# Clustered attention and two MLPs on one core: the first head pair in an older form, two low halves given to VectorE, and new order tables

## Chip, core and metric

The kernel runs on one core of a Trainium2 chip. The metric is the device time of one execution in microseconds (us), the median of three runs. Before the change it is 789.33 us.

## What is computed

```python
q_n, k_n, c_n = q / (|q| + 1e-6), k / (|k| + 1e-6), centroids / (|centroids| + 1e-6)
q_assign = argmax(einsum('bhsd,hcd->bhsc', q_n, c_n), -1)     # k_assign alike; 16 clusters
mask     = q_assign[:, :, :, None] == k_assign[:, :, None, :]
scores   = where(mask, q @ k.T / sqrt(D), -1e9)               # B, H, S, D = 2, 8, 768, 64
attn     = softmax(scores) @ v                                # written as x: 1536 tokens x 512
h = x @ w_in;  g = h * cos(h);                            x   = g @ w_out     # MLP1, 512-2048-512
h = x @ w_in2; g = where(h > 0, h, exp(min(h, 0)) - 1);   out = g @ w_out2    # MLP2
```

All of it is float32. TensorE multiplies fp32r values, so nearly every operand is split into a high half (a rounded copy) and a low half (operand minus high half), and three products stand for one: high by high, high by low, low by high.

## The kernel before

**Attention** goes by head pairs, two heads at a time, eight pairs in all. For a pair, the k and q rows are loaded, squared and summed, and their inverse norms come from three Newton steps on small tiles. TensorE transposes k and q, multiplies them with the normalised centroids (L874), and the argmax over 16 clusters is a chain of small VectorE and GpSimd operations on the tile `sm`: scale by the norm (L894), maximum (L902), compare (L909), keep the first (L918), a maximum again, and the one-hot tile `M` (L940). `M` is transposed and put beside k and q, so that the mask comes out of the score product itself (L1039, L1042). Each 128 queries are one step: scores, row maximum (L1047), exponential `P` (L1053), turn (L1062), halves `PH` and `PL` (L1076, L1082), times `V` (L1093). While a pair's six steps run, the next pair is prepared.

**The first pair** has no earlier pair to hide behind and has its own functions. `first_pe`, `first_hi`, `first_low` and `first_stack` make the stacked operands X0k, X0q (first head) and X1k, X1q (second head) from one transposed k or q. The centroids are normalised by `cen_sq`, fourteen small GpSimd operations (`cen_step`) and `cen_scale`. For the second pair, GpSimd and VectorE make the low halves `lo` (L742, L744), and SyncE copies the halves into X0k and X1k by DMA (L755 to L760).

**The MLPs.** The 1536 tokens are three token tiles of 512, t = 0, 1, 2. The hidden width is 16 slices f of 128. Token tile 0 goes slice by slice: `g1` (L221) is twelve matmuls giving h, `act` makes the activation and its halves GH and GL, `g2` (L280) is twelve matmuls into four accumulators. Token tiles 1 and 2 go by pairs p of slices (f = 2p and 2p+1) with seven half-size products (`prod`, L480) in place of eight, after which `post` combines them, and `act2` makes the activation and its halves. In MLP1 the activation is six operations on ScalarE and VectorE, then GH by ScalarE (L93) and GL by GpSimd (L544):

```python
        elif i == (5 if m == 0 else 3):
            copy_on(G2_ON[m][e][0], GH, A)
        else:
            eng = nc.vector if G2_ON[m][e][1] == "dve" else nc.gpsimd
            eng.tensor_tensor(out=GL, in0=A, in1=f32(GH), op=ALU.subtract)
```

Weights come from memory as 64-bit numbers. For each f, `load_w` (L144, L146) loads a raw tile through SyncE and `w_part` turns it into halves: ScalarE (L163), VectorE twice (L165, L167), then the high half (L93, L95 or L97, by engine) and the low half (L175) of a `slot`. The slot of a slice is used by all three token tiles of its MLP and then taken for the raw weights of the next. At the **boundary between the MLPs**, TensorE does the last `g2` slices of MLP1 (t = 2, f = 12 to 15) and the first `g1` slices of MLP2 in a written order. x is 512 wide, so four pieces of it are split too, XH (GpSimd, L97) and XL (VectorE, L202). The first two slots of MLP2 are made ahead in a guest place and only their halves remain.

**The order.** Every engine runs its instructions in order. Which stands where is not found by a scheduler: tables of numbers give each part a time, all parts are sorted by it, and written out in that order. FIRST holds the first pair, PAIR each later one, STEP, HALF and UNIT the attention steps, LAST the passage into MLP1, MLP and WINO the two forms of MLP tiles, WB the weight sums of the second form. OWN and the short tables ending in `_ON` name the engine of a part (MLP1's token tile 0 and the x halves above all).

## Time and profile before

| | |
|---|---|
| median of three runs | 789.33 us (786.51 to 790.74) |
| the profiled execution | 789.13 us, of which the span is 787.3 us; 1.83 us lie outside |
| TensorE matmuls (PE) | 766.7 us busy, 97% of the span |
| TensorE weight loads (PEld) | 686.5 us, beside the matmuls |
| VectorE (DVE) | 612.9 us, 78% |
| ScalarE (ACT) | 553.8 us, 70% |
| GpSimd (POOL) | 402.3 us, 51% |

The span is what the trace covers, from the first instruction to the last. Rows of the timeline give an instruction's start, its duration, its engine and line, what it writes and reads, and in brackets how long the engine had stood idle before it and who ended the idle time. Matmuls overlap, so those of 0.39 us start every 0.23 us. PEclk is the granted clock of TensorE as a share of 2.4 GHz.

The stages by time: to about 20 us the first pair is prepared, to 240 us attention runs, at 240 to 265 us attention passes into MLP1. MLP1's token tile 0 follows until about 350 us, and its tiles 1 and 2 until 521 us. The boundary between the MLPs is at 517 to 530 us, and MLP2 fills the rest.

### The profile page before, as it was taken

How to read it: one execution, taken by the hardware profiler on the slowest of the kernel's cores; microseconds unless marked ns; L12 is line 12 of the kernel's file. 1: busy time of each engine (PE TensorE's matmuls, PEld its weight loads, DVE VectorE, ACT ScalarE, POOL GpSimd, SP SyncE). 2: the span in 40 equal slices, each digit the busy share in tenths (PEclk: the TensorE clock that was granted, in tenths of full speed). 3: DMA queues.
4: the chain of work that ended last, by engine and by line, in shares of the span. 5: the costliest groups of instructions: out<-in, count | busy, mean ns of one | idle time of the engine just before them, and what ended most of it. 6: DMA issues, size and time to landing. Idle time of an engine off the chain costs nothing.

```text
span 787.3 us, 13051 instructions
## 1 busy us (share of the span) xinstructions
PE 766.7 (97%) x4579; PEld 686.5 (87%) x4579; DVE 612.9 (78%) x1008; ACT 553.8 (70%) x1035; POOL 402.3 (51%) x472
## 2 busy tenths in 40 slices
PE   6899999999999999999999999989999999999998
PEld 5789999999998878889999899968888999999996
DVE  6789899898899989989998844688978577663442
ACT  5788988989989988867666755766755554654343
POOL 7755866866865732444655422251228666532221
PEclk9899999999999999999999999999999999999999
DMA  5546657647437395011123238882000222223221
GB/s 122 121 98 154 147 117 161 138 104 182 101 87 267 39 374 210 1 40 61 62 81 121 71 113 285 292 275 102 0 1 25 110 81 82 81 95 120 81 80 54
DMA packets 72145, 93.27 MB, mean 118 GB/s; under 512 B 31440, under 2 KB 52432, under 8 KB 72080
## 3 DMA queue, kind: packets, MB, share of 16 engines
q1 hardware_dynamic: 71936, 92.41, 39.4%
q8 instruction: 36, 0.59, 0.3%
q14 instruction: 29, 0.24, 0.1%
q10 hardware_dynamic: 144, 0.03, 0.0%
HBM read 58.75 MB, written 15.78 MB: 95 GB/s over the span
## 4 chain that ended last, share of the span: by engine, by line
PE 91%; ACT 3%; POOL 2%; DVE 1%; DMA 1%; issue 1%; SPq 1%; ACTq 0%; POOLq 0%
PE a L280 32%; PE h L480 20%; PE h L221 11%; PE px L1093 8%; PE pt L1062 8%; PE s L1039 4%; PE s L1042 4%; PE pt_sim L874 2%; PE pt_raw L718 1%; ACT P L1053 1%; POOL GL L544 1%; ACT PH L1076 1%; DMA nat_q<-in_q_dram 1%; DMA X1k<-lo 1%; SPq L607 0%
## 5 line engine op out<-in xcount | busy, mean ns | idle before, releaser
L544 POOL TENSOR_TENSOR GL<-A,GH 128x512 fp32r<-128x512 f32 x64 | 93.3, 1463 | 155.2 <-ACT GH L93 118.4
L280 PE MATMUL a<-GH,slot 128*128 128x512 f32 x384 | 124.7, 393 | 0.0
L280 PE MATMUL a<-slot,GH 128*128 128x512 f32 x384 | 118.4, 389 | 0.0
L1082 DVE TENSOR_TENSOR PL<-pt,PH 128x384 fp32r<-128x384 f32 x192 | 99.0, 547 | 16.5 <-ACT PH L1076 16.5
L1076 ACT ACTIVATE PH<-pt 128x384 fp32r<-128x384 f32 x192 | 85.0, 496 | 18.5 <-PE pt L1062 18.3
L1047 DVE TENSOR_REDUCE m<-s 128x1 f32<-128x768 f32 x96 | 91.0, 948 | 4.2 <-PE s L1042 3.5
L1053 ACT ACTIVATE P<-s,m 128x768 f32<-128x768 f32 x96 | 87.3, 910 | 0.9 <-DVE m L1047 0.6
L280 PEld LDWEIGHTS a<-GH,slot 128*128 128x128 f32 x384 | 72.7, 189 | 14.8
L1062 PE MATMUL pt<-ident,P 128*128 128x128 f32 x576 | 84.2, 280 | 0.0
L221 PE MATMUL h<-XH,slot 128*128 128x512 f32 x256 | 83.7, 391 | 0.0
L280 PEld LDWEIGHTS a<-slot,GH 128*128 128x128 f32 x384 | 71.0, 188 | 14.0
L480 PE MATMUL h<-XH,slot 128*128 128x256 f32 x384 | 81.8, 282 | 0.0
L280 PE MATMUL a<-GL,slot 128*128 128x512 f32 x192 | 75.6, 394 | 3.7 <-POOL GL L544 3.7
L280 PE MATMUL a<-slot,GL 128*128 128x512 f32 x192 | 74.8, 389 | 0.0
L1062 PEld LDWEIGHTS pt<-ident,P 128*128 128x128 f32 x576 | 67.3, 142 | 6.3 <-DVE PL L1082 1.2
L93 ACT ACTIVATE GH<-A 128x512 fp32r<-128x512 f32 x86 | 53.9, 627 | 21.2 <-DVE A L539 9.3
L391 POOL TENSOR_TENSOR X<-slot 128x512 f32<-128x512 f32 x32 | 49.0, 1543 | 37.0 <-DVE sums L434 23.5
L480 PEld LDWEIGHTS h<-XH,slot 128*128 128x128 f32 x384 | 65.0, 190 | 0.7
L502 DVE TENSOR_TENSOR X<-X 128x256 f32<-128x256 f32 x32 | 23.4, 733 | 49.1 <-ACT X L500 48.9
L1093 PE MATMUL px<-PL,V 128*128 128x384 f32 x192 | 57.9, 356 | 0.7
L1093 PE MATMUL px<-PH,V 128*128 128x384 f32 x192 | 58.2, 357 | 0.0
L221 PEld LDWEIGHTS h<-XH,slot 128*128 128x128 f32 x256 | 48.2, 189 | 10.3 <-DVE slot L175 0.3
(197 smaller groups left out, 1958.6 us busy)
## 6 DMA issues: line engine op xcount, KB each, us to landing
raw<-in_moe_w_in_dram SPq DMA_DIRECT2D x32, 512.0 KB, 7.9
raw<-in_moe_w_out_dram SPq DMA_DIRECT2D x32, 512.0 KB, 8.8
sd<-sums SPq DMA_DIRECT2D x32, 384.0 KB, 2.3
sums<-sd SPq DMA_DIRECT2D x32, 384.0 KB, 3.5
nat_k<-in_k_dram SPq DMA_DIRECT2D x16, 192.0 KB, 3.3
nat_q<-in_q_dram SPq DMA_DIRECT2D x16, 192.0 KB, 3.8
nat_v<-in_v_dram SPq DMA_DIRECT2D x8, 384.0 KB, 4.4
xr<-row SPq DMA_DIRECT2D x32, 96.0 KB, 3.5
```

Of the source, the lines that this page charges most:

```text
L93: nc.scalar.activation(out=out, in_=in_, func=AF.Copy)
L221: nc.tensor.matmul(h, lhsT=a[:, kd, :], rhs=b, start=(kd == 0 and i == 0), stop=(kd == NKD - 1 and i == 2))
L280: nc.tensor.matmul(accs[m, t][e], lhsT=a, rhs=b, start=(f == 0 and i == 0), stop=(f == NF - 1 and i == 2))
L391: eng.tensor_tensor(out=u[:, i].rearrange("p e n -> p (e n)").rearrange("p (k f) -> p k f", k=NKD), in0=f32(ih), in1=f32(il), op=ALU.add)
L480: nc.tensor.matmul(o, lhsT=x[:, k], rhs=piece(y, k), start=(k == 0 and n == 0), stop=(k == 1 and n == 2))
L544: eng.tensor_tensor(out=GL, in0=A, in1=f32(GH), op=ALU.subtract)
L1047: nc.vector.tensor_reduce(out=m, in_=st[n]["s"][:, :, 0:HW], axis=AX.XY, op=ALU.max, negate=True)
L1053: nc.scalar.activation(out=P, in_=st[n]["s"][:, :, 0:HW], func=AF.Exp, bias=st[n]["m"], accum_out=den_all[:, u % NDEN, j, r, 0:1])
L1062: nc.tensor.transpose(pt[:, c * 128:(c + 1) * 128], st[n]["P"][:, e, c * 128:(c + 1) * 128], ident)
L1076: nc.scalar.activation(out=ph, in_=pt, func=AF.Copy)
L1082: nc.vector.tensor_tensor(out=pl, in0=pt, in1=f32(ph), op=ALU.subtract)
L1093: nc.tensor.matmul(tx[g][:, 0:HW], lhsT=V2s[pp][:, j, c, :], rhs=halves[g][a][:, c, :], start=(n == 0), stop=(n == 2 * C - 1))
```

## The change

Three things. **One:** the low halves GL of the last two pairs of MLP1 at t = 2 (f = 12 to 15, four instructions) are made by VectorE.

```diff
+G2_LATE = ((0,2,6), (0,2,7))
...
-            eng = nc.vector if G2_ON[m][e][1] == "dve" else nc.gpsimd
+            eng = nc.vector if G2_ON[m][e][1] == "dve" or (m, t, p) in G2_LATE else nc.gpsimd
```

**Two:** the first head pair. The centroid load goes on SyncE's queue ahead of k (it was on ScalarE's). The first pair's v is loaded ahead of the second head's k and q. The centroid's Newton steps are eleven VectorE operations (`norm_steps`) in place of GpSimd's. The low half X1q is VectorE's (it was GpSimd's, from a copy `fraw` by ScalarE), and T1k is ScalarE's (was VectorE's) and the copy X1k GpSimd's (was ScalarE's). GpSimd no longer halves the squares of the second head. VectorE does the second head's scale and keep-the-first (were GpSimd's).

```diff
-        nc.scalar.dma_start(out=cen[:, 0, :], in_=centroids.rearrange("h c d -> (h c) d"))
+        nc.sync.dma_start(out=cen[:, 0, :], in_=centroids.rearrange("h c d -> (h c) d"))
         for j in range(2):
             load_nat(0, "k", (j,))
             load_nat(0, "q", (j,))
-        load_nat(0, "v")
+            if j == 0:
+                load_nat(0, "v")
...
+        def norm_steps(key):
+            need(("seed", key))
+            ss, x, y, a = nt[key]
+            for _ in range(3):
+                nc.vector.tensor_tensor(out=a, in0=y, in1=y, op=ALU.mult)
+                nc.vector.scalar_tensor_tensor(out=a, in0=a, scalar=-0.5, in1=x, op0=ALU.mult, op1=ALU.mult)
+                nc.vector.scalar_tensor_tensor(out=y, in0=a, scalar=1.5, in1=y, op0=ALU.add, op1=ALU.mult)
+            nc.vector.tensor_tensor(out=y, in0=y, in1=ss, op=ALU.mult)
+            nc.vector.tensor_scalar_add(y, y, 1e-6)
...
-            if (w, j) == ("q", 1):
-                need(("fraw", w, j))
-                nc.gpsimd.tensor_tensor(out=xl, in0=raws_sb[0, w, j], in1=f32(th), op=ALU.subtract)
...
-            if js == (1,):
-                nc.gpsimd.tensor_tensor(out=sq[:, 1, :, 0:D // 2], in0=sq[:, 1, :, 0:D // 2], in1=sq[:, 1, :, D // 2:D],
-                                        op=ALU.add)
...
-            eng = nc.vector if js == (0,) else nc.gpsimd
+            eng = nc.vector if pp == 0 else nc.gpsimd
```

**Three:** all order tables have new numbers, and OWN new engines. In MLP1's token tile 0, the high halves of the weight slices 3, 7, 10 and 14 and the low half of slice 9 go to GpSimd, and so do GH of slices 9 and 15 and one XH; GpSimd gives up the high half of slice 8, GH of 5 and 10 and GL of 15. VectorE has three operations fewer there.

```diff
-STEP = {'qk': -0.7084, 'rowmax': -0.484, 'expo': 0.6444, 'turn:0': 1.5027, 'p_hi:0': 1.7761, 'p_lo:0': 2.025, 'turn:1': 1.6032, 'p_hi:1': 2.0128, 'p_lo:1': 2.2586}
+STEP = {'qk': -0.8439, 'rowmax': -0.5989, 'expo': 0.4499, 'turn:0': 1.4222, 'p_hi:0': 1.9292, 'p_lo:0': 2.1434, 'turn:1': 1.4486, 'p_hi:1': 1.9304, 'p_lo:1': 2.2468}
...
```

**VectorE at the boundary of the MLPs.** Before, from a middle row of the activation of f = 15 (tiles R_6693 and A_6644; those of f = 14 are R_6685 and A_6643) to the low half of MLP2's slot 2 (u is a weight on its way into a slot):

```order
L523 SCALAR_TENSOR_TENSOR R_6693<-R_6693,A_6644 128x512
L202 TENSOR_TENSOR XL_6664<-X_67,XH_6663 128x512
L533 TENSOR_TENSOR A_6643<-A_6643,R_6685 128x512
L202 TENSOR_TENSOR XL_6700<-X_67,XH_6699 128x512
L202 TENSOR_TENSOR XL_6691<-X_67,XH_6690 128x512
L165 TENSOR_SCALAR u_6717<-u_6717 128x1024
L533 TENSOR_TENSOR A_6644<-A_6644,R_6693 128x512
L175 TENSOR_TENSOR slot1_6728<-guest1_6633,slot1_6728 128x1024
L167 SCALAR_TENSOR_TENSOR u_6717<-raw2_6341,u_6717 128x1024
L165 TENSOR_SCALAR u_6749<-u_6749 128x1024
L175 TENSOR_TENSOR slot2_6751<-u_6717,slot2_6751 128x1024
```

In the change, from the same row (f = 14 is A_6642, f = 15 is A_6643):

```order
L524 SCALAR_TENSOR_TENSOR R_6690<-R_6690,A_6643 128x512
L176 TENSOR_TENSOR slot0_6668<-guest0_6518,slot0_6668 128x1024
L534 TENSOR_TENSOR A_6642<-A_6642,R_6686 128x512
L203 TENSOR_TENSOR XL_6658<-X_67,XH_6657 128x512
L203 TENSOR_TENSOR XL_6672<-X_67,XH_6671 128x512
L534 TENSOR_TENSOR A_6643<-A_6643,R_6690 128x512
L545 TENSOR_TENSOR GL_6688<-A_6642,GH_6687 128x512
L166 TENSOR_SCALAR u_6719<-u_6719 128x1024
L168 SCALAR_TENSOR_TENSOR u_6719<-raw2_6225,u_6719 128x1024
L545 TENSOR_TENSOR GL_6692<-A_6643,GH_6691 128x512
L176 TENSOR_TENSOR slot1_6723<-guest1_6600,slot1_6723 128x1024
```

GL_6688 and GL_6692 stand in VectorE's queue behind the last A and ahead of the low half of slot 1, with two rows of slice 2 between them. Behind these rows VectorE also makes the high halves of slots 2 and 3, which it did not before.

**GpSimd at the boundary.** Before, from the GL of f = 12 on:

```order
L544 TENSOR_TENSOR GL_6575<-A_6530,GH_6574 128x512
L544 TENSOR_TENSOR GL_6581<-A_6531,GH_6580 128x512
L97 TENSOR_SCALAR XH_6663<-X_67 128x512
L97 TENSOR_SCALAR XH_6690<-X_67 128x512
L97 TENSOR_SCALAR XH_6699<-X_67 128x512
L544 TENSOR_TENSOR GL_6687<-A_6643,GH_6686 128x512
L544 TENSOR_TENSOR GL_6695<-A_6644,GH_6694 128x512
L97 TENSOR_SCALAR slot2_6751<-u_6717 128x1024
L263 TENSOR_TENSOR GL_6768<-A_6765,GH_6767 128x512
```

In the change:

```order
L545 TENSOR_TENSOR GL_6466<-A_6425,GH_6465 128x512
L545 TENSOR_TENSOR GL_6470<-A_6426,GH_6469 128x512
L98 TENSOR_SCALAR XH_6653<-X_67 128x512
L98 TENSOR_SCALAR XH_6657<-X_67 128x512
L98 TENSOR_SCALAR XH_6664<-X_67 128x512
L98 TENSOR_SCALAR XH_6671<-X_67 128x512
L264 TENSOR_TENSOR GL_6758<-A_6755,GH_6757 128x512
```

The four GL after GL_6470 and slot 2's high half are gone from here, and one XH more stands in their place; the next row is a GL of MLP2.

**TensorE and GpSimd in the first pair.** TensorE before, from the scores of the fourth step (`s`) to those of the fifth; X0k and X1k here are the second pair's, whose low halves arrive by DMA:

```order
L1039 MATMUL s_454<-X0k_177,X0q_202 128x384 x2
L1042 MATMUL s_454<-T0k_179,T0q_204 128x384 x2
L874 MATMUL pt_sim_460<-CC_152,X0k_359 128x32 x4
L1062 MATMUL pt_465<-ident_121,P_436 128x128 x3
L1062 MATMUL pt_471<-ident_121,P_436 128x128 x3
L874 MATMUL pt_sim_460<-CC_152,X0k_359 128x32 x2
L874 MATMUL pt_sim_460<-CC_152,X1k_360 128x32
L1039 MATMUL s_493<-X0k_177,X0q_202 128x384 x2
L1042 MATMUL s_493<-T0k_179,T0q_204 128x384 x2
```

In the change:

```order
L1034 MATMUL s_446<-X0k_167,X0q_196 128x384 x2
L1037 MATMUL s_446<-T0k_169,T0q_198 128x384 x2
L869 MATMUL pt_sim_452<-CC_152,X0k_345 128x32 x2
L869 MATMUL pt_sim_452<-CC_152,X1k_346 128x32 x2
L1057 MATMUL pt_461<-ident_121,P_430 128x128 x3
L1057 MATMUL pt_465<-ident_121,P_430 128x128 x3
L869 MATMUL pt_sim_452<-CC_152,X0k_345 128x32
L869 MATMUL pt_sim_452<-CC_152,X1k_346 128x32 x2
L869 MATMUL pt_sim_452<-CC_152,X0k_345 128x32
L1034 MATMUL s_485<-X0k_167,X0q_196 128x384 x2
L1037 MATMUL s_485<-T0k_169,T0q_198 128x384 x2
```

A product with X1k now stands right behind the first with X0k, ahead of the turn (`pt`). GpSimd, before, ahead of the second pair's first `lo`:

```order
L996 TENSOR_SCALAR V2_332<-nat_v_113 128x6x64
L894 TENSOR_TENSOR sm_266<-sm_266,nrm_189 128x2x96
L830 TENSOR_TENSOR sq_350<-nat_k_115 128x768
L835 TENSOR_TENSOR sq_350<-sq_350 128x12x32
L838 TENSOR_TENSOR sq_350<-sq_350 128x12x16
L918 TENSOR_TENSOR sm_266<-sm_266,desc_128 128x2x96
L742 TENSOR_TENSOR lo_364<-raw_371,hi_363 128x384
```

In the change:

```order
L675 TENSOR_SCALAR ny_264<-ny_264 128x12
L828 TENSOR_TENSOR sq_358<-nat_k_115 128x768
L830 TENSOR_TENSOR sq_358<-sq_358 128x12x32
L833 TENSOR_TENSOR sq_358<-sq_358 128x12x16
L752 TENSOR_TENSOR lo_350<-raw_362,hi_349 128x384
L828 TENSOR_TENSOR sq_406<-nat_q_118 128x768
```

The V copy, the scale and the keep-the-first (the two rows on `sm`) no longer stand ahead of `lo`.

## Rows read from the trace of the kernel before

**Rows 1.** The page, busy time of TensorE: busy us, share of the span, instructions

```profile
PE 766.7 (97%) x4579; PEld 686.5 (87%) x4579; DVE 612.9 (78%) x1008; ACT 553.8 (70%) x1035; POOL 402.3 (51%) x472
```

**Rows 2.** The page, the chain that ended last, shares of the span by engine

```profile
PE 91%; ACT 3%; POOL 2%; DVE 1%; DMA 1%; issue 1%; SPq 1%; ACTq 0%; POOLq 0%
```

**Rows 3.** Windows: stretch, its us, each engine's busy us, PEclk, DMA share, GB/s

```profile
60.00:240.00 180.00, 179.43 (x1252) 169.33 (x1251) 162.34 (x319) 165.10 (x381) 122.56 (x194) 1.00 0.59 137
265.00:425.00 160.00, 160.00 (x858) 138.44 (x857) 149.56 (x216) 118.72 (x190) 72.98 (x49) 1.00 0.32 111
530.00:784.00 254.00, 253.53 (x1439) 223.14 (x1437) 163.12 (x239) 137.14 (x227) 104.23 (x72) 1.00 0.19 69
526.00:530.00 4.00, 4.00 (x12) 3.15 (x11) 2.42 (x3) 1.15 (x2) 1.55 (x2) 0.57 0.98 351
31.00:39.00 8.00, 7.80 (x35) 7.51 (x36) 5.16 (x9) 4.21 (x10) 4.59 (x16) 0.57 0.68 146
285.00:325.00 40.00, 40.00 (x178) 32.89 (x177) 39.93 (x51) 32.31 (x45) 8.23 (x6) 1.00 0.56 200
```

**Rows 4.** Waits of TensorE: total us, times, longest us

```profile
PE a L280 <- POOL GL L544: 3.7, 1, 3.7
...
PE pt_c L693 <- DVE cen L687: 1.6, 1, 1.6
```

**Rows 5.** Timeline of TensorE at the boundary of the MLPs

```profile
525.34 0.50 PE L280 MATMUL a<-GL,slot 128*128 128x512 f32 x1 [3.66 <-POOL GL L544]
```

**Rows 6.** Timeline of GpSimd: the GL of f = 14 and 15

```profile
519.71 6.83 POOL L544 TENSOR_TENSOR GL<-A,GH 128x512 fp32r<-128x512 f32 x2 [4.30 <-ACT GH L93]
```

**Rows 7.** Tile GL, 495 to 530 us: ns min/median/max, first and last start

```profile
L544 POOL TENSOR_TENSOR GL<-A,GH x6: 1283/1297/5581, 497.6 to 525.3; 128x512 fp32r<-128x512 f32 x6
```

**Rows 8.** Timeline of VectorE at the boundary

```profile
517.61 0.68 DVE L202 TENSOR_TENSOR XL<-X,XH 128x512 fp32r<-128x512 f32 x1
...
520.62 0.68 DVE L533 TENSOR_TENSOR A<-A,R 128x512 f32<-128x512 f32 x1
521.22 1.21 DVE L175 TENSOR_TENSOR slot<-guest,slot 128x1024 fp32r<-128x1024 f32 x1
```

**Rows 9.** Timeline of TensorE in the first pair

```profile
28.55 0.59 PE L874 MATMUL pt_sim<-CC,X0k 128*128 128x32 f32 x4 [1.31 <-DMA X0k<-lo]
...
31.20 0.25 PE L874 MATMUL pt_sim<-CC,X1k 128*128 128x32 f32 x1 [1.21 <-DMA X1k<-lo]
```

**Rows 10.** Timeline of GpSimd in the first pair

```profile
14.70 1.81 POOL L801 TENSOR_TENSOR X1q<-fraw,T1q 64x768 fp32r<-64x768 f32 x1
...
19.98 0.51 POOL L996 TENSOR_SCALAR V<-nat_v 128x384 fp32r<-128x384 f32 x1
20.45 0.52 POOL L894 TENSOR_TENSOR sm<-sm,nrm 128x192 f32<-128x192 f32 x1
...
24.11 0.58 POOL L918 TENSOR_TENSOR sm<-sm,desc 128x192 f32<-128x192 f32 x1
24.65 1.00 POOL L742 TENSOR_TENSOR lo<-raw,hi 128x384 fp32r<-128x384 f32 x1
```

**Rows 11.** SyncE's queue: first load, and the copy that X1k waits for

```profile
0.73 0.39 SPq L607 DMA_DIRECT2D nat_k<-in_k_dram  x1
...
26.88 0.59 SPq L758 DMA_DIRECT2D X1k<-lo  x1
```

**Rows 12.** Timeline of VectorE in the first pair

```profile
13.70 0.95 DVE L804 SCALAR_TENSOR_TENSOR X1k<-s_raw,T1k 64x768 fp32r<-64x768 f32 x1
...
17.15 0.36 DVE L909 TENSOR_TENSOR sm<-sm,mx 128x192 f32<-128x192 f32 x1
...
21.39 1.22 DVE L909 TENSOR_TENSOR sm<-sm,mx 128x192 f32<-128x192 f32 x1
```

**Rows 13.** Timeline of TensorE: g1 of two slices of MLP1 that follow each other

```profile
296.21 0.39 PE L221 MATMUL h<-XH,slot 128*128 128x512 f32 x1
...
301.65 0.39 PE L221 MATMUL h<-XH,slot 128*128 128x512 f32 x1
```

More of the change, by code (lines that the diff above doesn't have):

```diff
@@ L28 @@
-STEP = {'qk': -0.7084, 'rowmax': -0.484, 'expo': 0.6444, 'turn:0': 1.5027, 'p_hi:0': 1.7761, 'p_lo:0': 2.025, 'turn:1': 1.6032, 'p_hi:1': 2.0128, 'p_lo:1': 2.2586}
-HALF = {'av:0:0': 6.7513, 'av:0:1': 6.3384, 'av:1:0': 6.9826, 'av:1:1': 4.8875, 'av:2:0': 5.1627, 'av:2:1': 6.3004, 'av:3:0': 4.7675, 'av:3:1': 4.6933, 'av:4:0': 4.8112, 'av:4:1': 4.6976, 'av:5:0': 4.8024, 'av:5:1': 6.8253, 'x_main': 7.2376, 'x_low': 7.0237}
-UNIT = {'den_eps': 2.8361, 'recip': 3.7535, 'recip_rows': 6.6707, 'recip_out': 8.4112, 'x_add': 9.2483, 'x_mul': 17.2906}
@@ new lines @@
+STEP = {'qk': -0.8439, 'rowmax': -0.5989, 'expo': 0.4499, 'turn:0': 1.4222, 'p_hi:0': 1.9292, 'p_lo:0': 2.1434, 'turn:1': 1.4486, 'p_hi:1': 1.9304, 'p_lo:1': 2.2468}
+HALF = {'av:0:0': 6.2719, 'av:0:1': 4.8074, 'av:1:0': 4.7218, 'av:1:1': 4.4542, 'av:2:0': 6.276, 'av:2:1': 4.9696, 'av:3:0': 4.6165, 'av:3:1': 6.4759, 'av:4:0': 4.979, 'av:4:1': 6.5822, 'av:5:0': 5.1983, 'av:5:1': 6.4762, 'x_main': 7.0575, 'x_low': 6.9662}
+UNIT = {'den_eps': 2.7037, 'recip': 3.2698, 'recip_rows': 5.4033, 'recip_out': 8.9866, 'x_add': 8.4622, 'x_mul': 16.7153}
@@ L43 @@
 ABS2_ON = ("act", "act")
+G2_LATE = ((0, 2, 6), (0, 2, 7))
 GUEST = {(1, 0): 9, (1, 1): 10}
@@ L49 @@
 RAW_ON = {('k', 0): 'act', ('k', 1): 'dve', ('q', 0): 'act', ('q', 1): 'act'}
-HI2_ON = {('k', 0): 'act', ('k', 1): 'act', ('q', 0): 'act', ('q', 1): 'act'}
+HI2_ON = {('k', 0): 'act', ('k', 1): 'pool', ('q', 0): 'act', ('q', 1): 'act'}
 ZON = {'z': 'act', **{(w, h, j): 'dve' if (w, h) == ('k', 1) else 'act' for w in 'kq' for h in range(2) for j in range(2)}}
@@ L54 @@
 SQ0_ON = {('k', 0): 'act', ('k', 1): 'act', ('q', 0): 'act', ('q', 1): 'act'}
-TH_ON = {('k', 0): 'act', ('k', 1): 'dve', ('q', 0): 'act', ('q', 1): 'act'}
+TH_ON = {('k', 0): 'act', ('k', 1): 'act', ('q', 0): 'act', ('q', 1): 'act'}
 WHI_ON = {0: 'act', 1: 'act'}
@@ L649, in norm_seed @@
             made("seed", key)
+        def norm_steps(key):
[7 more added lines that the diff above has]
+            nc.vector.tensor_scalar_add(y, y, 1e-6)
+            made("steps", key)
         def norm_step(key, i):
@@ L679, in cen_sq @@
             norm_seed("c", css, "c")
-        def cen_step(i):
-            norm_step("c", i)
         def cen_scale():
@@ L787, in first_hi @@
             made("th", w, j)
-        def first_raw(w, j):
-            raw = raws_sb[0, w, j] = pre.tile([64, 2, HW], F32, tag="fraw", bufs=1, name="fraw")
-            src, sc, *_ = first_parts(w, j)
-            nc.scalar.activation(out=raw, in_=src, func=AF.Copy, scale=sc)
-            made("fraw", w, j)
         def first_low(w, j):
@@ L798, in first_low @@
             src, sc, th, xh, xl = first_parts(w, j)
-            if (w, j) == ("q", 1):
-                need(("fraw", w, j))
-                nc.gpsimd.tensor_tensor(out=xl, in0=raws_sb[0, w, j], in1=f32(th), op=ALU.subtract)
-                made("low", w, j)
-                return
             nc.vector.scalar_tensor_tensor(out=xl, in0=src, scalar=sc, in1=f32(th), op0=ALU.mult, op1=ALU.subtract)
@@ L846, in sum_sq @@
             nc.vector.tensor_reduce(out=sss[pp][:, "kq".index(w), cols(js)],
-                                    in_=sqs[pp, w, js][:, cols(js), :, 0:(D // 2 if js == (1,) else D if pp == 0 or SS_ON[w] == "dve" else D // 4 if SSQ == "quarter" else D // 2)],
+                                    in_=sqs[pp, w, js][:, cols(js), :, 0:(D if pp == 0 or SS_ON[w] == "dve" else D // 4 if SSQ == "quarter" else D // 2)],
                                     axis=AX.X, op=ALU.add)
@@ L916, in sims_first @@
             sm = sims_of(pp, js)
-            eng = nc.vector if js == (0,) else nc.gpsimd
+            eng = nc.vector if pp == 0 else nc.gpsimd
             eng.tensor_tensor(out=sm, in0=sm, in1=desc.unsqueeze(1).unsqueeze(1).to_broadcast(list(sm.shape)),
@@ L1199 @@
                 fn, own = named(name)
-                if fn in (first_pe, first_hi, first_raw, first_low, first_hi2, first_stack):
+                if fn in (first_pe, first_hi, first_low, first_hi2, first_stack):
                     at(time, fn, *own, j)
@@ L1203 @@
                     at(time, fn)
-                elif fn is cen_step:
+                elif fn is norm_steps:
                     at(time, fn, *own)
```

14 lines of the change are left out of this document (7 added, 7 removed).

## The prediction

> **What bounds the kernel now.** I read the page first. TensorE computes in 766.7 us of a span of 787.3 us [rows 1], so 20.6 us of idle time is all that an order can win, apart from time at a lower clock. The chain that ended last is TensorE for 91% [rows 2]. A change that moves work among the other engines pays only where TensorE waits for that work, and costs only where it makes TensorE wait. So I looked by stage for idle time. Steady attention leaves 0.57 us in 180, the MLP1 stretch none in 160, MLP2 0.47 us in 254 [rows 3]. What is left lies at the two ends of the order: the first pair, and the boundary of the MLPs.
>
> At the boundary there is one wait of 3.66 us for a low half GL by GpSimd [rows 4, 5]. The reader should see why it is long. GL has a median of 1.30 us, and the one that TensorE waits for took 5.58 [rows 7]; it begins at 519.71 [rows 6], with VectorE's operations back to back beside it [rows 8]. The second of the two rows grouped there took only about 1.25 us. After the wait TensorE works at a granted clock of 0.57 for 4 us [rows 3], between the levels 2.4 and 1.2 GHz, having been idle just before. That costs 4 x (1 - 0.57) = 1.7 us more. In the first pair the second pair's keys come late by DMA, with waits of 1.31 and 1.21 us [rows 9], and behind them 8 us pass at 0.57 [rows 3], or 8 x 0.43 = 3.4 us lost.
>
> **The change part by part.** The sum starts from the profiled execution, 789.13 us, of which 1.83 lie outside the span.
>
> *The two late GL.* They leave GpSimd for VectorE. For one on VectorE the nearest row is a subtraction of the same shape and kinds, 0.68 us, of which a run of them starts every 0.6 [rows 8]. Where they stand decides. Before, A of f = 15 starts at 520.62 [rows 8]; one weight row of 0.6 that stood ahead of it is behind it now, and slot 0's low half has only changed places within the run. So A ends at about 520.7 and the GL of f = 14 at about 521.4. TensorE wants it 3.66 us ahead of 525.34, at 521.68 [rows 5]. Allowing for the wait on GH, the remaining stall is 0 to 0.4; I take 0.3. Two rows of slice 2 follow (together about 1.8), then the GL of f = 15, done at 523.9 to 524.3. TensorE comes to it one g2 later. A slice's g1 and g2 together take 301.65 - 296.21 = 5.44 us [rows 13], so g2 half of that, and the need is at 521.68 + 2.7 = 524.4. Slot 1's low half takes 1.21 [rows 8] and ends by 525.5. Its need, after both g2, is about 521.5 + 5.4 = 526.9. All hold, the tightest by 0.1 us. The gain is 3.66 - 0.3 = 3.4, the bounds 0 and 3.66. With no idle time of that size ahead of it, I expect no fall of the clock: 1.7 more, the bounds 0 and 1.7.
>
> *What GpSimd no longer does there* covers nothing else: it stands idle 4.30 us ahead of these GL [rows 6]. The extra XH fits in that.
>
> *The second pair's keys.* GpSimd's `lo` starts at 24.65. The V copy, 0.51, the scale, 0.52, and the keep-the-first, 0.58, leave its queue, 1.6 us in all, and X1q, 1.81, makes place for a plain copy [rows 10]. I take 2.0, since behind that `lo` waits for ScalarE's halves. The DMA copy X1k, issued at 26.88 [rows 11], should follow and land at about 29.2, not 31.2 [rows 9]. But TensorE now asks for X1k right behind X0k, before the turn, and not behind it. It came to X0k at 28.55 - 1.31 = 27.24 [rows 9], so one idle stretch of 29.2 - 27.24 = 2.0 us takes the place of 1.31 + 1.21 = 2.5: a gain of 0.5. Bounds: a loss of 1.4, if X1k lands no earlier (31.20 - 27.24 = 4.0 in place of 2.5, with the turn behind it), and a gain of 2.5. The clock loss of 3.4 may go with it or stay; since an idle stretch remains, I leave it in the sum.
>
> *The head up to the first scores.* The centroid load ahead of k on SyncE's queue puts k about 0.39 later [rows 11]. Against it, the centroid's Newton steps leave GpSimd for VectorE, and VectorE's X1q is a row of 0.95 [rows 12] in place of GpSimd's 1.81 [rows 10]; VectorE gives up T1k, whose row is of the same size. The wait for the centroid is 1.6 [rows 4]. I take 0. The best is half the centroid's wait, a gain of 0.8; the worst is k's delay and a second delay of the same order from v ahead of the second head, a loss of 1.0.
>
> *The second head's small operations on VectorE.* The compare L909 took 0.36 us at 17.15 and 1.22 at 21.39 [rows 12], the second time beside GpSimd's work on squares. Two more such operations now stand in VectorE's queue beside the squares, ahead of the first row maximum. I take 0, since the squares can also begin later or earlier; the bound is 0.9, one such difference. The Trainium skill's page "SBUF — State Buffer", section "SBUF: two separate sides", says that a VectorE operation with two SBUF inputs and a GpSimd one exclude each other for a whole instruction. By that rule the second head would lose those 0.9 us for certain, and the sum would be 784.4 in place of 783.5; the two prices of L909 agree with the rule, as does the GL of 5.58 us.
>
> *All other tables.* Steady attention, MLP1 and MLP2 have 0.57, 0 and 0.47 us to win [rows 3]. I take 0, with a gain of 1.0 and a loss of 3 as bounds, the loss being one new wait of the size of the boundary's without its clock.
>
> The sum: 789.13 - 3.4 - 1.7 - 0.5 = 783.5 us. The profiled execution is 0.2 below the median of the runs, so for the median I say **783.7 us**. About 0.5%, 3.9 us, is what a measurement of this kernel can tell from no change, so faster means under 785.4 and slower over 793.3.
>
> **The rivals.**
>
> *A: the clock holds in the first pair too.* If the granted clock stays at 1.00 behind the one stretch of idle time, the 3.4 come on top: 783.7 - 3.4 = 780.3. For it: one stretch in place of two. Against it: about 2.0 us of idle time remain, near the 2.5 behind which the clock fell.
>
> *B: the stall moves into VectorE's queue.* GL now waits behind A, XL and slot rows. If A is 1.5 to 2.5 us later than walked, since the sine is later on ScalarE, TensorE waits about 2.0 in place of 0.3, the clock falls as before and the 1.7 stay: 783.7 + 2.0 - 0.3 + 1.7 = 787.1, with a spread of 786 to 788.5, which is no change. For it: margins of 0.1 us; behind the GL on VectorE stand the low halves of slots 1 to 3, for which the first g1 of MLP2 wait. Against it: the times of the walk are VectorE's own of before [rows 8], and only 0.68 us for each GL is new in its queue.
>
> *C: slower, by GpSimd starved in MLP1's token tile 0.* From 285 to 325 us VectorE is busy in 39.93 of 40 us and GpSimd in 8.23 [rows 3]. The change gives GpSimd seven more pieces in that tile, and if they stand beside VectorE as the GL at the boundary did, each takes up to 5.58 - 1.30 = 4.3 us more. A slice has 5.44 us. Where GpSimd's end comes after TensorE's need, a wait like the boundary's follows, 3.66 + 1.7 = 5.4 us; two such waits give 783.7 + 10.7 = 794.4. It decides from the second late piece on. For it: the saturated VectorE. The exclusion that the Trainium skill's page "SBUF — State Buffer" states would bear on this too, wherever both read two operands at once. Against it: 31 us of GpSimd's idle time in these 40, and VectorE has three operations fewer there.
>
> **How the numbers follow.** The forecast has 0.50: its own range, with the head and the tables at part of their bounds, is 781.5 to 785.4. A has 0.15, B 0.25, C 0.10. Faster is the forecast and A, 0.65; within 0.5% is B, 0.25; slower is C, 0.10. The range holds the forecast, A and B: 780.0 to 788.5. It leaves out C and the ends of A and B.
>
> **What would show it.** At the boundary the wait of TensorE for GL should be gone or under 0.5 us, with VectorE as its releaser, and the granted clock 1.00 where it was 0.57. In the first pair, one wait for X1k, none for X0k behind the turn, and `lo` near 23 us. In the windows of attention and of both MLPs, TensorE's idle time should not grow by over a microsecond. The forecast is wrong if TensorE waits for a slot or for GL on VectorE (B), if there are waits in MLP1's first token tile for GpSimd's slot or GH (C), or if the first scores come over 1 us later.

## The result, and the profile after

| | before | changed |
|---|---|---|
| median | 789.34 us (786.51 to 790.74, 4 runs) | **778.12 us** (777.81 to 778.32, 4 runs) |
| ratio | | 0.9862, 95% interval 0.9835 to 0.9889 |
| profiled execution, span | 789.13, 787.3 us | 778.07, 776.3 us |

The change is faster by 11.2 us, twice the 5.6 that were forecast, and 1.9 us below the range. This is a difference of medians. Beside the experiments below, the kernel before ran 71 times more, from 780.8 to 791.5 us; seven of these, 780.8 to 781.8 us, have a mean granted clock of 1.000, about 3 us above the changed kernel at such a clock (777.8 to 778.3 us at 0.999 to 1.000). So most of the gain seems to lie in waits and stretches of lower clock that the kernel before has in most of its executions, but not in all. None of the seven was profiled; the rows of before come from an execution that has them. The page of the changed kernel, busy time and then the chain by engine:

```profile
PE 761.6 (98%) x4579; PEld 682.2 (88%) x4579; DVE 631.8 (81%) x1026; ACT 548.0 (71%) x1030; POOL 387.0 (50%) x453
...
PE 86%; DVE 6%; ACT 4%; DMA 2%; issue 1%; SPq 0%; POOL 0%; ACTq 0%; DVEq 0%
```

The same matmuls take 5.1 us less than in [rows 1], as much as the two stretches of lower clock cost before (1.7 + 3.4). The rest of the 11 us of span is idle time. The waits of TensorE, total us, times, longest:

```profile
PE pt_sim L869 <- DMA X1k<-lo: 1.1, 2, 0.5
...
PE pt_c L703 <- DVE cen L697: 0.7, 1, 0.7
...
PE pt_sim L869 <- ACT hi L737: 0.6, 1, 0.6
...
PE pt_sim L869 <- DMA X1q<-lo: 0.4, 1, 0.4
```

GL is not among them, and the centroid has 0.7 us in place of 1.6 [rows 4]. Windows of the changed kernel (stretch, its us, busy us of PE, PEld, DVE, ACT and POOL, PEclk, DMA share, GB/s): attention, MLP1, MLP2, and the 8 us in the first pair where the clock had been low:

```profile
60.00:240.00 180.00, 178.30 (x1237) 167.07 (x1235) 163.09 (x314) 164.52 (x375) 124.63 (x195) 1.00 0.60 144
265.00:425.00 160.00, 160.00 (x872) 139.41 (x871) 148.38 (x210) 116.45 (x184) 75.89 (x53) 1.00 0.33 116
525.00:773.00 248.00, 247.50 (x1413) 218.12 (x1411) 175.34 (x239) 131.72 (x222) 104.78 (x72) 1.00 0.20 72
28.00:32.00 4.00, 3.47 (x30) 3.38 (x28) 3.48 (x8) 3.78 (x9) 3.05 (x11) 1.00 1.05 216
32.00:36.00 4.00, 4.00 (x33) 3.75 (x30) 3.41 (x6) 3.83 (x8) 1.04 (x5) 1.00 1.00 167
```

Against [rows 3], attention has 1.1 us more idle time (two new waits for DMA copies, 0.43 and 0.51 us, are in it), the MLPs none, and the granted clock is 1.00 where it was 0.57. TensorE in the first pair, first scores and products of the second pair's keys, and then its first low half on GpSimd and the DMA copy of X1k on SyncE's queue:

```profile
18.61 0.99 PE L1034 MATMUL s<-X0k,X0q 128*128 128x384 f32 x2
...
26.41 0.40 PE L869 MATMUL pt_sim<-CC,X0k 128*128 128x32 f32 x2 [0.55 <-ACT hi L737]
27.35 0.36 PE L869 MATMUL pt_sim<-CC,X1k 128*128 128x32 f32 x2 [0.54 <-DMA X1k<-lo]
```

```profile
21.23 1.00 POOL L752 TENSOR_TENSOR lo<-raw,hi 128x384 fp32r<-128x384 f32 x1
```

```profile
23.56 0.59 SPq L768 DMA_DIRECT2D X1k<-lo  x1
```

The first scores stood at 19.85 us before. `lo` is 3.4 us earlier than in [rows 10] and X1k's copy 3.3 earlier than in [rows 11], and the two waits ahead of the products are 1.1 us where they were 2.5 [rows 9]. Only the second of them is still for a key's DMA copy; the first ends with a copy by ScalarE (`hi`). The scores of the fifth step start at 28.64, 2.66 us earlier than before, and the second pair's first scores at 48.98, where before they stood at 55.26. So the sum of the profiled executions is: 1.24 us to the first scores, 1.42 more to the fifth step and 3.62 more behind it, where the clock had been low, 6.3 in all; 3.66 + 1.7 at the boundary of the MLPs; 0.36 for a wait for XL in MLP1 that is gone; less 0.94 for the two new waits in attention. That makes 11.1, and 789.13 - 778.07 is 11.1.

VectorE at the boundary, changed kernel:

```profile
514.73 0.69 DVE L545 TENSOR_TENSOR GL<-A,GH 128x512 fp32r<-128x512 f32 x1
...
516.06 1.23 DVE L168 SCALAR_TENSOR_TENSOR u<-raw,u 128x1024 uint32<-128x1024 uint32 x1
517.20 0.69 DVE L545 TENSOR_TENSOR GL<-A,GH 128x512 fp32r<-128x512 f32 x1
517.80 1.22 DVE L176 TENSOR_TENSOR slot<-guest,slot 128x1024 fp32r<-128x1024 f32 x1
```

A GL takes 0.69 us here, and TensorE's first product with the GL of f = 14 starts at 516.05 without a wait: 0.6 us of slack, where the forecast had a wait of 0.3.

### The profile page after: what moved, and what is told of

Read it like the earlier page. It is cut to its first block, busy times and chain, and to the rows that moved or that the text cites. A ratio compares the mean times of both kernels' runs of the same rounds, so it can differ in the third digit from the quotient of the medians.

```text
span 776.3 us, 13062 instructions
## 1 busy us (share of the span) xinstructions
PE 761.6 (98%) x4579; PEld 682.2 (88%) x4579; DVE 631.8 (81%) x1026; ACT 548.0 (71%) x1030; POOL 387.0 (50%) x453
## 4 chain that ended last, share of the span: by engine, by line
PE 86%; DVE 6%; ACT 4%; DMA 2%; issue 1%; SPq 0%; POOL 0%; ACTq 0%; DVEq 0%
PE a L281 32%; PE h L481 20%; PE h L222 11%; PE pt L1057 6%; PE px L1088 6%; PE s L1034 3%; PE s L1037 3%; PE pt_sim L869 2%; DVE m L1042 2%; DVE PL L1077 1%; DMA X1k<-lo 1%; PE pt_raw L728 1%; ACT PH L1071 1%; DMA X1q<-lo 1%; ACT P L1048 1%
## 5 line engine op out<-in xcount | busy, mean ns | idle before, releaser
L545 POOL TENSOR_TENSOR GL<-A,GH 128x512 fp32r<-128x512 f32 x60 | 81.1, 1357 | 150.5 <-ACT GH L94 118.6
L281 PE MATMUL a<-GH,slot 128*128 128x512 f32 x384 | 122.9, 390 | 0.0
L481 PE MATMUL h<-XH,slot 128*128 128x256 f32 x384 | 79.2, 281 | 0.0
L501 ACT ACTIVATE X<-h 128x512 f32<-128x512 f32 x32 | 19.1, 597 | 54.2 <-PE h L481 54.0
L1088 PE MATMUL px<-PL,V 128*128 128x384 f32 x192 | 56.2, 368 | 0.0
```

The costliest lines, as they stand in the source:

```text
L281: nc.tensor.matmul(accs[m, t][e], lhsT=a, rhs=b, start=(f == 0 and i == 0), stop=(f == NF - 1 and i == 2))
L481: nc.tensor.matmul(o, lhsT=x[:, k], rhs=piece(y, k), start=(k == 0 and n == 0), stop=(k == 1 and n == 2))
L1088: nc.tensor.matmul(tx[g][:, 0:HW], lhsT=V2s[pp][:, j, c, :], rhs=halves[g][a][:, c, :], start=(n == 0), stop=(n == 2 * C - 1))
```

## Experiments

The kernel before ran beside each. Its own executions spread from 780.8 to 791.5 us, with mean granted clocks of 0.980 to 1.000 over the run, so each ratio below has an interval of about 0.3 to 0.6% either way.

### The boundary of the MLPs: GL alone, GL undone, GL seven times

**GL on VectorE alone.** The kernel before with

```diff
+G2_LATE = ((0,2,6), (0,2,7))
-            eng = nc.vector if G2_ON[m][e][1] == "dve" else nc.gpsimd
+            eng = nc.vector if G2_ON[m][e][1] == "dve" or (m, t, p) in G2_LATE else nc.gpsimd
```

> The kernel before with the four GL of f = 12 to 15 on VectorE alone; they stand where the old tables put them, behind the last A and ahead of slot 1's low half. Theory (the wait of 3.7 us was GpSimd's GL running beside VectorE): that wait gone or under 0.5 us, granted clock 1.00 behind it: 789.3 - 5 = 784.3 us. Rival (the wait moves to the slots, whose low halves now stand behind two more operations on VectorE, so that only the new tables make it pay): a wait of 1.5 to 3 us for a slot and the lower clock: 787 to 789 us.

784.95 us, ratio 0.9965 (0.9934 to 0.9996). TensorE at the boundary:

```profile
519.69 0.50 PE L281 MATMUL a<-GL,slot 128*128 128x512 f32 x1 [0.74 <-DVE GL L545]
```

The wait goes from 3.66 to 0.74 us, a little over the 0.5 expected, and the granted clock behind it is 1.00. The theory held, and no slot was waited for. Over the ten executions it is the upper end that goes, 785.9 where the kernel before reaches 791.1 in this series; the lowest, 781.88, is not below its lowest, 780.77.

The profiled execution is that lowest one, and it shows something else. With the old first pair and the old tables it has no wait for X0k or X1k, and a granted clock of 1.00 from 24 to 40 us. Six turns, and then the first products of the second pair's keys, here and (last row) the same turns before the change:

```profile
25.80 1.49 PE L1063 MATMUL pt<-ident,P 128*128 128x128 f32 x6
...
28.68 0.62 PE L875 MATMUL pt_sim<-CC,X0k 128*128 128x32 f32 x4
```

```profile
25.39 0.82 PE L1062 MATMUL pt<-ident,P 128*128 128x128 f32 x6
```

The same turns take 1.49 us here and 0.82 before, both at a granted clock of 1.00 on the page. TensorE came to X0k at 28.68, where before it came at 27.24 and had to wait. So the waits for the keys, and the lower clock behind them, are not in every execution of the old first pair either.

**GL back on GpSimd in the changed kernel**, `G2_LATE = ()`:

> The changed kernel with the four GL back on GpSimd. VectorE is busy in 14.97 of 15 us at this place in the changed kernel. Theory: GpSimd's GL takes 4 to 6 us beside it and TensorE waits 3.5 us or more, with a granted clock near 0.5 behind: 778.1 + 5.4 = 783.5 us or more. Rival (the new tables alone, with VectorE's and ScalarE's rows earlier, removed the wait): a wait under 1 us, 778 to 779.5 us.

780.6 us, ratio 0.9898 (0.986 to 0.9936). The timelines of GpSimd, VectorE and TensorE:

```profile
516.18 4.38 POOL L545 TENSOR_TENSOR GL<-A,GH 128x512 fp32r<-128x512 f32 x2 [5.48 <-ACT GH L94]
```

```profile
517.23 2.19 DVE L168 SCALAR_TENSOR_TENSOR u<-raw,u 128x1024 uint32<-128x1024 uint32 x1
519.35 2.31 DVE L176 TENSOR_TENSOR slot<-guest,slot 128x1024 fp32r<-128x1024 f32 x1
```

```profile
518.39 0.50 PE L281 MATMUL a<-GL,slot 128*128 128x512 f32 x1 [0.61 <-POOL GL L545]
```

Here the rival was nearer: a wait of 0.61 us, not 3.5. GpSimd starts no earlier: 1.6 us ahead of TensorE's need (518.39 - 0.61 - 516.18), before the change 2.0. But the two GL take 4.4 us in place of 6.8, and the first is done after 2.2, not after 5.6. VectorE's rows stand in another order here; which of them lets GpSimd in was not taken apart. In these profiles either half of the change takes most of the wait away, and with both it is gone. But the order alone doesn't decide it. The run with the products later in the kernel before, further down, has everything at the boundary as before, and in its profile GpSimd got in: the GL took 1.53 us, not 5.58, though it starts 0.90 us behind the same VectorE row as in [rows 6], and a VectorE row of 0.68 us took 1.78. TensorE waited for no GL.

```profile
531.25 1.53 POOL L544 TENSOR_TENSOR GL<-A,GH 128x512 fp32r<-128x512 f32 x1 [4.30 <-ACT GH L93]
```

```profile
531.56 1.78 DVE L165 TENSOR_SCALAR u<-u 128x1024 uint32<-128x1024 uint32 x1
```

So which engine gets in first differs between executions of one order, and what GL on VectorE takes away is the chance of the long wait. The other 2 us of this kernel over 778.12 are in the first pair (the clock, below), which the edit doesn't touch. In the rows of this kernel VectorE pays as well: two of its operations take 2.19 and 2.31 us here, 1.23 and 1.22 in the changed kernel. This agrees with the rule of exclusion that the Trainium skill's page "SBUF — State Buffer", section "SBUF: two separate sides", states; by the rows it strikes whichever engine comes second.

**GL of f = 14 seven times in the changed kernel**, six of them for nothing:

```diff
+            for _ in range(7 if (m, t, f) == (0, 2, 14) else 1):
-            eng.tensor_tensor(out=GL, in0=A, in1=f32(GH), op=ALU.subtract)
+                eng.tensor_tensor(out=GL, in0=A, in1=f32(GH), op=ALU.subtract)
```

> The changed kernel with the GL of f = 14 written seven times by VectorE in place of once, 3.6 us more ahead of TensorE's need, which had 0.6 us of slack in the profile of the change. Theory (an idle time of about 3 us at the boundary brings the lower clock behind it, as before the change): a wait of 3.0 us, granted clock of 0.5 to 0.6 over some 4 us behind it, 3 + 1.7 = 4.7 us slower than the changed kernel beside it. Rival (the clock falls there for another reason): 3 us slower, granted clock 1.00.

785.87 us, ratio 0.9971 (0.9937 to 1.0006). TensorE at the boundary, and the window behind:

```profile
523.22 0.79 PE L281 MATMUL a<-GL,slot 128*128 128x512 f32 x1 [3.62 <-DVE GL L546]
```

```profile
524.00:526.00 2.00, 2.00 (x7) 1.52 (x6) 2.00 (x3) 0.00 (x0) 0.00 (x0) 0.50 0.00 0
```

A wait of nearly the old length, now made by another engine, brings the lower clock back. The fastest of its executions, 782.36, is 5.3 us above the fastest of the changed kernel in the same series (777.07), close to the price of the wait and the clock before, 3.66 + 1.7. The medians lie further apart, 7.6 us; the difference is again the clock in the first pair, 0.50 from 28 to 36 us in this profile.

### The first pair and the steady tables

**The first pair alone**: the kernel before with the change's first pair and FIRST, all else old.

> The kernel before with the first head pair's form and its table FIRST alone from the change; all other tables and the boundary between the MLPs stay as before. Theory (the gain of some 6.2 us before 55 us comes from the first pair's form, which frees GpSimd's queue ahead of the low halves): the first scores 1.2 us earlier, the waits for X0k and X1k down from 2.5 to about 1.1 us, the granted clock at 1.00 from 31 to 39 us; about 789.3 - 6 = 783 us. Rival (the steady table PAIR, which places the second pair's low halves earlier, brings the shorter wait and with it the clock): the first scores still 1.2 us earlier, but waits near 2.5 us and a granted clock near 0.57 behind them remain: about 788 us. Either way the wait of 3.7 us for GL at the boundary stays.

786.14 us, ratio 0.9948 (0.9919 to 0.9978), the runs in two groups, 780.2 to 781.4 and 785.9 to 788.1. In the profile no wait for X0k or X1k is left. That agrees with the first pair's form, but doesn't decide, since the profile with GL alone has none either. The wait for GL is there, 3.7 us; the gap between the two groups, 5.4 us from middle to middle, is as long as its price with the clock, but no execution of the lower group was profiled. The median is 3 us above the expected. Windows:

```profile
12.00:16.00 4.00, 4.00 (x21) 4.00 (x20) 3.74 (x10) 1.65 (x2) 3.10 (x12) 0.50 0.16 35
...
28.00:32.00 4.00, 3.18 (x25) 2.85 (x25) 3.93 (x10) 3.52 (x8) 2.58 (x8) 1.00 0.93 200
...
523.00:527.00 4.00, 3.96 (x9) 3.14 (x10) 1.73 (x2) 0.68 (x2) 2.23 (x2) 0.50 1.00 313
```

The clock is 1.00 from 28 us on, as expected, but in this execution it fell earlier (0.50 from 12 to 24 us), behind waits of 4.15 and 0.99 us for the loads of k, and it still falls at the boundary.

**The steady tables alone**: the kernel before with PAIR, STEP, HALF and UNIT of the change.

> The kernel before with the tables of steady attention (PAIR, STEP, HALF, UNIT) alone from the change. Theory (first pair's form): waits near 2.5 us for X0k and X1k and a granted clock near 0.57 remain: 788 to 790.5 us, with the two new waits of 0.4 and 0.5 us for the DMA copies at steady pairs. Rival (PAIR): one wait of 1 to 2 us, granted clock 1.00 behind it: 784 to 786 us.

801.6 us, ratio 1.017 (1.0114 to 1.0225), slower than anything expected. The waits for X0k and X1k are 2.64 and 2.17 us; further waits stand ahead of the third pair (1.95 us for its load) and at the passage into MLP1 (2.2 and 1.68 us), where the old LAST stands beside new tables. So the rival fell; the size says little of the change.

**The old first pair in the changed kernel**: the old form and FIRST, all else new.

> The changed kernel with the old form of the first head pair and the old table FIRST; everything else is the change's, the boundary too. Theory (the first pair's form brings the early keys of the second pair): waits for X0k and X1k of 4 to 5 us together, as in the run with the steady tables alone, first scores at about 19.9 us, granted clock near 0.5 behind: 778.1 + 1.2 + 3.5 + 3.4 = 786 us, up to 788. Rival (the boundary and the matching tables bring nearly all): 779 to 781 us.

791.28 us, ratio 1.0039 (1.0009 to 1.007): the whole gain is lost, and more, 3 us beyond the expected range. TensorE:

```profile
29.67 0.37 PE L875 MATMUL pt_sim<-CC,X0k 128*128 128x32 f32 x2 [2.61 <-DMA X0k<-lo]
32.21 0.58 PE L875 MATMUL pt_sim<-CC,X1k 128*128 128x32 f32 x2 [2.17 <-DMA X1k<-lo]
...
58.89 0.62 PE L719 MATMUL pt_raw<-ident,nat_k 128*128 128x128 f32 x3 [2.04 <-DMA nat_k<-in_k_dram]
```

The new tables ask for the second pair's keys sooner than the old first pair can give them, and the third pair's load comes late in its turn.

**First pair and GL under the old tables**: the changed kernel with PAIR, STEP, HALF, UNIT, LAST, MLP, OWN, WINO and WB as before.

> The changed kernel with all order tables but FIRST as before: the new first pair and the four GL on VectorE, in the old steady order. Theory (these two parts are the change's gain, and the new tables add only what they save in front of the MLPs' boundary and lose in steady attention): the sum of the two parts measured alone, 789.2 - 3.05 - 4.2 = 782 us, or less where the clock holds, and within 2 us of the changed kernel's 778 to 780. Rival (the new tables are worth more than 3 us by themselves, the earlier low halves of the second pair above all): 783 us or more, with the clock falling in the first pair in nearly every run.

781.85 us (781.68 to 782.35), ratio 0.9943 (0.9917 to 0.9969). The theory held. From the medians: 784.95 with GL alone, 781.85 with the first pair too, 778.1 to 780.3 with the new tables too. The tables are thus worth 1.5 to 3.7 us, but only on the new first pair; on the old one they cost 6.

What the new first pair brings under the old tables is the narrow spread: twelve executions within 0.7 us, where those with GL alone went from 781.9 to 785.9. The lowest hardly move. The profiles agree. First scores of the second pair, with GL alone (the execution without waits for the keys) and in this run:

```profile
52.21 0.51 PE L1040 MATMUL s<-X0k,X0q 128*128 128x384 f32 x2
```

```profile
52.13 0.51 PE L1034 MATMUL s<-X0k,X0q 128*128 128x384 f32 x2
```

Before they stood at 55.26, in the change at 48.98. So about half of the 6.3 us that these two profiles differ by at this place, 3.1, is what the old first pair also saves in an execution without the waits and the lower clock; the other half, 3.2, came with the new tables on the new first pair.

### The first scores

**No halving of the squares**, in the kernel before:

```diff
-            if js == (1,):
-                nc.gpsimd.tensor_tensor(out=sq[:, 1, :, 0:D // 2], in0=sq[:, 1, :, 0:D // 2], in1=sq[:, 1, :, D // 2:D],
-                                        op=ALU.add)
...
-    0:(D // 2 if js == (1,) else D if pp == 0
+    0:(D if pp == 0
```

> The kernel before with GpSimd's halving of the second head's squares left out and the sums made by VectorE over the full width; nothing else. Theory (VectorE's sum waited 2.07 us for that halving, and the centroid's scaling stood behind it): the scaled centroid and the first scores 0.7 to 1.0 us earlier, at about 19.0 us, the time 0 to 1 us lower. Rival (the centroid's own steps on GpSimd set it): first scores at 19.7 us or later.

788.46 us, ratio 1.0 (0.997 to 1.003). TensorE:

```profile
9.18 0.47 PE L693 MATMUL pt_c<-ident,cen 128*128 128x128 f32 x1 [0.68 <-DVE cen L687]
...
18.70 0.99 PE L1036 MATMUL s<-X0k,X0q 128*128 128x384 f32 x2
...
27.43 0.59 PE L871 MATMUL pt_sim<-CC,X0k 128*128 128x32 f32 x4 [1.35 <-DMA X0k<-lo]
30.05 0.36 PE L871 MATMUL pt_sim<-CC,X1k 128*128 128x32 f32 x1 [1.05 <-DMA X1k<-lo]
```

From the first transpose (which waits for k) to the first scores it is 15.23 us here, 16.29 before, 14.90 in the change: of the 1.39 us gained, 1.06 come from this one edit. But the waits for the keys stay, and the clock falls behind them, to 0.50 from 32 to 36 us. A microsecond at the end can't be told from none here: 788.46 against 789.39 beside it.

**The centroid's Newton steps on GpSimd again**, in the changed kernel, ahead of the V copy:

```diff
 def norm_steps(key):
-    ...
+    for i in range(4):
+        norm_step(key, i)
```

> The changed kernel with the centroid's Newton steps on GpSimd again (fourteen operations, ahead of the V copy). Theory (VectorE comes to the scaled centroid only at 8.4 us, behind X0k and two sums, and GpSimd is done at about 7.2): nothing moves, first scores at 18.6 us, 778.1 us within 0.4 either way. Rival (the steps on VectorE are what brought the first scores 1.2 us forward): first scores 0.8 us later or more, 779 us or more.

780.02 us, ratio 0.9872 (0.9842 to 0.9903); the changed kernel ran at 780.32 in this series. From first transpose to first scores it is 14.89 us (18.98 - 4.09), as in the change: VectorE comes to the centroid later than either engine is done with it. Once the halving is gone, the steps' place is worth nothing. Before, it was not so clear. VectorE's wait for the halving, and the halving on GpSimd:

```profile
9.13 0.35 DVE L846 TENSOR_REDUCE ss<-sq 128x6 f32<-128x192 f32 x1 [2.07 <-POOL sq L832]
```

```profile
8.51 1.13 POOL L832 TENSOR_TENSOR sq<-sq 128x192 f32<-128x192 f32 x2
```

The halving stands right behind the centroid's steps in GpSimd's queue. Whether moving the steps with the halving kept would have freed it as well was not tried.

### The second pair's keys and the clock

**The changed kernel again**, in two more series:

> The changed kernel itself once more, beside the others of this series. The kernel with GL back on GpSimd has the same first pair, yet its runs had a mean granted clock of 0.990 to 0.996 and its profile 0.87 and 0.76 from 20 to 40 us. Theory (the first pair of the change leaves idle time so short that the clock falls only in some executions): runs from 778 to 781.5 us, some with a mean clock of 0.99 or more below 1.00. Rival (the clock never falls there; the fall belonged to the other kernel): all runs within 777.5 to 778.7 us at 0.999 to 1.000.

> The changed kernel itself, for the comparison with the run of its later products in the same series. Theory: either 778 to 778.5 us with a mean clock of 0.999 or more, or 780 to 781.3 with a lower one, by whether the clock falls in the first pair. Rival: times between these without relation to the clock.

First 780.32 us (780.01 to 781.26), ratio 0.9885 (0.985 to 0.9919), mean clocks 0.986 to 0.995; then 778.25 us (777.07 to 780.59), ratio 0.9886 (0.9842 to 0.9931), clocks 0.989 to 1.000. Windows of the first of the two:

```profile
28.00:32.00 4.00, 4.00 (x26) 3.90 (x24) 2.84 (x6) 2.73 (x7) 2.95 (x10) 0.65 1.02 212
32.00:36.00 4.00, 4.00 (x19) 3.60 (x18) 1.98 (x3) 3.19 (x7) 1.13 (x5) 0.50 1.05 175
```

The same program, with waits of 0.55 and 0.89 us ahead of the products in place of 0.55 and 0.54, lost its clock there and ended 2 us later. So the 3.4 us are not safely gone with the change; in some executions some 2 us of them come back. The expectation of the second run held only in part: its two fastest executions, 777.07 and 777.11 us, have a mean clock of 0.991, below that of slower ones at 777.91 (1.000) and 778.60 (0.998). Where the clock falls matters more than whether it does.

**The low half two microseconds later**, in the changed kernel (the second pair's first `lo` on GpSimd written three times):

```diff
+                for _ in range(3 if (pp, w, half) == (1, "k", 0) else 1):
```

> The changed kernel with the second pair's first low half written three times by GpSimd in place of once, so that the DMA copies of X0k and X1k start 2 us later. Theory (the idle time for the second pair's keys is what brings the lower clock behind it): waits for X0k and X1k of about 3 us together in place of 1.1, granted clock near 0.5 to 0.6 over some 8 us behind them, 778.1 + 2 + 3.4 = 783.5 us. Rival (the clock falls by chance or for another reason): waits of 3 us, granted clock 1.00, 780 us.

782.75 us, ratio 0.9914 (0.9885 to 0.9944), 2.4 us over the changed kernel in the same series. TensorE:

```profile
27.25 0.39 PE L870 MATMUL pt_sim<-CC,X0k 128*128 128x32 f32 x2 [1.91 <-DMA X0k<-lo]
29.03 0.58 PE L870 MATMUL pt_sim<-CC,X1k 128*128 128x32 f32 x2 [1.39 <-DMA X1k<-lo]
```

The waits grow from 1.44 to 3.30 us, the clock is 0.50 from 28 to 36 us. But in this series it had fallen without the edit too, so this prices the wait (1.9 us of it cost 2.4) and doesn't tell why the clock falls. In this execution it had been at 0.50 from 12 to 20 us as well. Windows:

```profile
12.00:16.00 4.00, 4.00 (x21) 4.00 (x20) 3.77 (x9) 1.17 (x2) 3.13 (x11) 0.50 0.00 0
...
28.00:32.00 4.00, 2.97 (x14) 3.00 (x15) 3.14 (x8) 1.47 (x3) 2.73 (x8) 0.50 0.98 236
```

**The products later, in the kernel before**: PAIR's `sims_pe:k` 0.2 to 0.6 of a step later.

> The kernel before with the products of the next pair's keys 0.2 to 0.6 of a step later in the table PAIR, so that a turn and a step's scores stand ahead of them; nothing else. Theory (the 2.5 us of idle time for the second pair's keys bring the clock's fall in the first pair): the waits down to 1 us or less, granted clock 1.00 from 31 to 39 us in most executions, 2 to 5 us faster than the kernel before, 784 to 787 us. Rival (the clock falls in the first pair by its idle time before 20 us as well, so that taking these waits away only moves the fall): the waits down, a clock of 0.5 in another stretch, within 2 us of the kernel before.

797.2 us, ratio 1.0164 (1.0112 to 1.0215). The waits for X0k and X1k are gone, but waits of 0.61 and 1.63 us for PL stand in their place, the clock falls elsewhere (0.50 from 12 to 20 us, and 0.69 from 32 to 36), and one wait of 8.85 us came up at the start of MLP1, whose origin was not followed. The time says nothing of the clock, and on that the run is inconclusive. Its boundary is the one shown above, with no wait for GL.

**The products later, in the changed kernel**: four entries of PAIR, 0.3 of a step.

```diff
-'sims_pe:k:3': 2.1987, 'sims_pe:k:0': 2.2136, 'sims_pe:k:8': 2.246, 'sims_pe:k:7': 2.4106
+'sims_pe:k:3': 2.4987, 'sims_pe:k:0': 2.5136, 'sims_pe:k:8': 2.546, 'sims_pe:k:7': 2.7106
```

> The changed kernel with TensorE's first four products of the next pair's keys (X0k, X1k) 0.3 of a step later in the table PAIR, so that a turn stands ahead of them, in every pair. Theory (these short waits are what is left, and the clock falls behind them where they come together): the two waits of the first pair down from 1.1 to 1.4 us to about 0.5, the waits for X1k in later pairs gone, a fall of the clock at 28 to 36 us rarer: 0.6 to 3 us faster than the changed kernel run beside it. Rival (the first pair is bound by ScalarE's and VectorE's queues and the turn's time only moves): within 0.4 us of it.

777.33 us (776.93 to 779.57), ratio 0.9874 (0.9831 to 0.9918): the lowest median of all, 0.9 us under the changed kernel beside it, which the intervals can't tell apart. No wait for a DMA copy of the keys is left, in any pair. Windows:

```profile
12.00:16.00 4.00, 4.00 (x20) 4.00 (x20) 3.75 (x9) 1.06 (x2) 3.18 (x12) 0.50 0.00 0
...
32.00:36.00 4.00, 4.00 (x33) 3.79 (x31) 3.63 (x7) 3.84 (x9) 1.08 (x5) 1.00 0.99 164
```

Here the granted clock is at its lower level from 12 to 20 us and the mask product still comes at 17.54 (17.50 in the change at 1.00). The rows tell why. A group of products at this place, here and in the change:

```profile
15.36 1.44 PE L869 MATMUL pt_sim<-CC,X1k 128*128 128x32 f32 x6
```

```profile
15.33 1.44 PE L869 MATMUL pt_sim<-CC,X1k 128*128 128x32 f32 x6
```

They take as long at 1.00 as at 0.50. In the change, too, the two scores of a step take 0.99 us at 18.61 and 0.62 at 24.89, and the page has 1.00 at both. So up to some 23 us, 28 in the run with GL alone, a granted clock of 1.00 on the page doesn't mean that TensorE ran at the speed of later rows, and the lower clock at 12 to 20 us can't be priced against it.

## Why the prediction was wrong

*The boundary* was right in sum: 3.4 + 1.7 forecast, 3.66 + 1.7 measured, with GL alone (ratio 0.9965) and GL seven times (5.3 us between the fastest) bearing the price out. That the whole price shows in the result is in part luck: the profile that the forecast started from has the wait, and the GL of 1.53 us above shows that it is not there in every execution. The seven executions at 780.8 to 781.8 us point the same way. In its profile the changed kernel with GL on GpSimd leaves 0.61 us of the wait, and GL alone leaves 0.74. The walk put the GL of f = 14 at TensorE's need or 0.3 us behind; it came 0.6 ahead.

*The head up to the first scores* was taken at 0, with a gain of 0.8 as its best, and measured 1.24. The term was looked for in the wrong place. The walk weighed the Newton steps and X1q; what held the centroid was VectorE's sum of the second head's squares, queued ahead of it and waiting 2.07 us for GpSimd's halving, which itself stood behind the Newton steps. The diff removes both from GpSimd. The run without the halving shows 1.06 us.

*The second pair's keys* was the failing step. Their idle stretch was put at 2.0 us, with X1k landed at 29.2 and TensorE at X0k at 27.24. X1k landed 1.9 us earlier than that, at 27.3, and TensorE came 1.4 earlier, at 25.86; the two first products with X0k fill 0.4 of the stretch. The waits measured 1.1. And "since an idle stretch remains, I leave it in the sum": the 3.4 us of the clock did not stay. That was rival A, at 0.15. At 780.3 it missed the measured 778.12 by the first scores (1.2) and the shorter waits (0.9); the smaller items about cancel. The step took the waits and the lower clock of one execution for those of every one. By the further series, whether the clock falls there is open in each execution of the changed kernel (778.1, 780.3 and 778.3 us were its medians), and the run with GL alone shows it open in the old first pair too. What decides it is not settled. The profiles show one thing that differs ahead of it, the time at which TensorE's rows become shorter (from 0.99 to about 0.6 us for two scores), but no run sets that time.

*The rule of exclusion* had put the second head's small operations 0.9 us later for certain. The compare took 0.67 us, against 0.36 alone and 1.22 beside the squares [rows 12], and the first row maximum came at 20.71, where it had stood at 22.53.

*Rival B*: no wait for VectorE at the boundary of the changed kernel; with the old tables 0.74 us. *Rival C*: MLP1's window has TensorE busy in 160.00 of 160 us, as before. Its seven more pieces for GpSimd are four, eight less the four that it gives up. *All other tables* were taken at 0, with 1.0 as the most to win, from windows that begin at 60 us. But the same tables order the steps of the first pair, and there they are worth about 3 us on its new form (52.13 to 48.98). The term also hid 0.9 us of new waits in attention, and a dependence on the new first pair (791.28 us without it).
